# Laying model-width vectors with 8 neighbours in a partition: longer weight runs, column loads of x and c, and a result stored from columns

## Chip, cores and metric

One core of a Trainium2 chip. The metric is the device time of one execution in microseconds (us); executions of one kernel agree within about 0.3%. The time lies about 1.8 us above the span that the profile shows. The profiled run of the kernel before is one of its slowest (444.45 us, span 442.7); its usual span is 442.0 to 442.6.

## The reference, cut to what matters

One decoding step of a transformer block for one token. The model width D is 1024. The work is a modulation, attention over a cache of 65,536 positions with 4 key/value heads, and a gated feed-forward layer; every weight is read once.

```python
mod = silu(c) @ w_mod                                  # w_mod 1024 x 6144
sa, ca, ga, sb, cb, gb = six chunks of 1024
h = layernorm(x) * (1 + ca) + sa
x = x + ga * (attention(h @ wq, k_cache, v_cache) @ wo)  # wq 1024 x 4096, wo 4096 x 1024
h = layernorm(x) * (1 + cb) + sb
x = x + gb * ((gelu(h @ w_gate) * (h @ w_up)) @ w_down)  # 1024 x 3584, twice; 3584 x 1024
```

All arrays are bf16, together 185.6 MB, of which the caches are 134 MB.

## The kernel before

Weights and cache tiles go through ten slots of 16 KB per partition in SBUF, the core's working memory of 128 partitions. One queue of loads runs as far ahead as free slots allow.

```python
x_row = sb("x_row", [KD, P], dt.bfloat16)      # KD = 8, P = 128
c_row = sb("c_row", [KD, P], dt.bfloat16)
# ... some thirty further tiles ...
y_col = sb("y_col", [P, KD])
y_row = sb("y_row", [KD, P], dt.bfloat16)
# ...
slots = [nc.alloc_sbuf_tensor(f"slot{i}", [P, SLOT], dt.bfloat16) for i in range(NSLOT)]
```

The slots come after all the small tiles.

A vector of width 1024 lies so that element `128*k + p` is in partition `p`, column `k`. The rows of a weight matrix are loaded to match, and a product is made block by block: a 128 x 128 piece of weights is the stationary operand and one column of the vector moves, giving 128 results in the partitions.

```python
wq_v = A_wq.rearrange("(k p) n -> p k n", p=P)
# ...
def matvec(bank, jobs, rhs, ready, nblk, pick=None, first=True):
    PE.wait(*ready)
    for (jb, view, k0, nk) in jobs:
        PE.wait(jb.tok)                                  # the tile has landed
        for kk in range(nk):
            for j in range(nblk):
                w = pick(view, kk, j) if pick else view[:, kk, j * P:(j + 1) * P]
                ins = pe.matmul(bank[:, j:j + 1], w, rhs[:, k0 + kk:k0 + kk + 1], ...)
        tok = PE.done(ins)
        release(jb, tok)                                 # the slot may be loaded again
```

Gate and up already use a `pick` that takes every fourth column of the weights. The end of the kernel turns the result from columns to 8 rows and stores those:

```python
v = matvec(acc_bank["dn"], j_d, u_col, (v_uc,), KD)
# ... t_dn = dn * gb; y_col = t_dn + x1_col ...
v = PE.done(pe.transpose(b6[0:KD, 384:384 + P], y_col[:, :], identf[:, :]))
v = DVE.done(dve.tensor_copy(y_row[:, :], b6[0:KD, 384:384 + P]))
sp.dma_start(out[0, 0].rearrange("(j p) -> j p", p=P), y_row[:, :])
```

## Time and profile before

| | before |
|---|---|
| median time | 443.99 us (443.78 to 444.12, 3 runs) |
| DMA packets, bytes | 15,392, 186.08 MB |
| DMA rate from 60 to 360 us | 430 GB/s |
| last full down tile can be used at | 436.83 us |
| end of span | 442.7 us |

The page of the kernel before. The second and third lines cut the span into 40 slices: the busy share of the core's 16 DMA engines in tenths, then GB/s. The last two are the chain of waits that ended last.

```profile
span 442.7 us, 16779 instructions
...
DMA  8999999999999999999999999999999999999994
GB/s 329 429 423 426 434 431 426 429 427 421 432 429 432 426 427 437 432 429 428 434 434 430 429 429 433 431 434 429 429 434 431 432 429 428 423 424 424 427 425 177
DMA packets 15392, 186.08 MB, mean 420 GB/s; under 512 B 1536, under 2 KB 1536, under 8 KB 3840
...
DMA 75%; PE 20%; issue 2%; DVE 1%; SPq 1%; ACT 1%
```

There is no slice without DMA work. The kernel moves bytes all the time, and everything else only matters if it changes how fast or how early the bytes move, or if it follows the last bytes.

The timeline of the tensor engine in the feed-forward layer: start and duration in us, engine, line, output and operands, count, and in brackets how long the engine had been idle and what ended that.

```profile
392.59 2.02 PE L316 MATMUL kt_ps<-h_col,slot 128*128 128x1 bf16 x56 [2.01 <-DVE h_col L363]
...
426.74 1.84 PE L316 MATMUL kt_ps<-u_col,slot 128*128 128x1 bf16 x64 [3.03 <-DMA slot<-in_B_w_down_dram]
```

The first line is one gate tile, with weight columns 4 apart: 56 matmuls in 2.02 us. One matmul lasts 172 ns, but they overlap; from start to start it is (2.02 - 0.172) / 55, or about 34 ns. The second is a down tile with neighbouring columns: (1.84 - 0.165) / 63, or 27 ns.

The end of the same timeline:

```profile
436.83 2.29 PE L316 MATMUL kt_ps<-u_col,slot 128*128 128x1 bf16 x80 [3.45 <-DMA slot<-in_B_w_down_dram]
439.28 0.58 PE L316 MATMUL kt_ps<-u_col,slot 128*128 128x1 bf16 x16 [0.15 <-DMA slot<-in_B_w_down_dram]
439.90 0.17 DVE L664 TENSOR_TENSOR t_dn<-kt_ps,mod_sb 128x8 f32<-128x8 f32 x1 [15.91 <-PE kt_ps L316]
440.10 0.17 DVE L666 TENSOR_TENSOR y_col<-t_dn,x_col 128x8 f32<-128x8 f32 x1
440.32 0.38 PE L668 MATMUL b<-identf,y_col 128*8 128x128 f32 x1 [0.46 <-DVE y_col L666]
440.74 0.28 DVE L670 CAST y_row<-b 8x128 bf16<-8x128 f32 x1 [0.47 <-PE b L668]
441.04 0.37 SPq L672 DMA_DIRECT2D out_dram<-y_row  x1
```

After the last full down tile there are 96 matmuls (the last 16 wait for the last small tile), then 1.14 us from the first vector instruction to the issue of the store, and 1.6 us from there to the end of the span.

Two waits in the timeline and in the wait list, which the change touches: x and c landed at 6.79 us, and the last wait of the store queue (in all, times, longest) was for the store to land.

```profile
6.79 0.16 PE L296 MATMUL b<-ident,c_row 8*128 8x8 bf16 x1 [6.79 <-DMA x_row<-in_A_x_dram]
```

```profile
SPq L676 <- DMA out_dram<-y_row: 0.9, 1, 0.9
```

### The profile page before, as it was taken

How to read it: one execution, taken by the hardware profiler on the slowest of the kernel's cores; microseconds unless marked ns; L12 is line 12 of the kernel's file. 1: busy time of each engine (PE TensorE's matmuls, PEld its weight loads, DVE VectorE, ACT ScalarE, POOL GpSimd, SP SyncE). 2: the span in 40 equal slices, each digit the busy share in tenths (PEclk: the TensorE clock that was granted, in tenths of full speed). 3: DMA queues.
4: the chain of work that ended last, by engine and by line, in shares of the span. 5: the costliest groups of instructions: out<-in, count | busy, mean ns of one | idle time of the engine just before them, and what ended most of it. 6: DMA issues, size and time to landing. Idle time of an engine off the chain costs nothing.

```text
span 442.7 us, 16779 instructions
## 1 busy us (share of the span) xinstructions
PE 335.0 (76%) x7849; PEld 325.2 (73%) x7849; DVE 164.8 (37%) x282; ACT 143.1 (32%) x548; POOL 3.8 (1%) x21
## 2 busy tenths in 40 slices
PE   1333468898979899989899988979898974654434
PEld 1333458898979899979799987969898964654434
DVE  1000046544536445544644644554544443210000
ACT  1000013444444333634533453543343562000000
POOL 2000000000000000000000000000000000000000
PEclk9999999867788956967955996895967785555555
DMA  8999999999999999999999999999999999999994
GB/s 329 429 423 426 434 431 426 429 427 421 432 429 432 426 427 437 432 429 428 434 434 430 429 429 433 431 434 429 429 434 431 432 429 428 423 424 424 427 425 177
DMA packets 15392, 186.08 MB, mean 420 GB/s; under 512 B 1536, under 2 KB 1536, under 8 KB 3840
## 3 DMA queue, kind: packets, MB, share of 16 engines
q1 hardware_dynamic: 15328, 185.61, 98.5%
q8 instruction: 25, 0.41, 0.3%
q14 instruction: 7, 0.06, 0.0%
q10 hardware_dynamic: 32, 0.00, 0.0%
HBM read 185.60 MB, written 0.00 MB: 419 GB/s over the span
## 4 chain that ended last, share of the span: by engine, by line
DMA 75%; PE 20%; issue 2%; DVE 1%; SPq 1%; ACT 1%
DMA slot<-in_A_v_cache_dram 55%; PE kt_ps L417 9%; DMA slot<-in_A_wq_dram 8%; DMA slot<-in_B_w_up_dram 6%; DMA slot<-in_B_w_down_dram 6%; PE b L481 5%; PE sc_ps L437 3%; PE kt_ps L316 1%; SPq L212 1%; PE b L461 1%; ACT p_sb L547 1%; PE b L451 1%; DVE kt_sb L612 0%; PE b L621 0%; DVE zs L597 0%
## 5 line engine op out<-in xcount | busy, mean ns | idle before, releaser
L417 PE MATMUL kt_ps<-ident,slot 128*128 128x128 bf16 x2048 | 171.9, 252 | 4.9 <-DMA slot<-in_A_k_cache_dram 3.0
L516 DVE COPY kt_sb<-kt_ps 128x2048 bf16<-128x2048 bf16 x96 | 117.5, 1225 | 100.0 <-PE kt_ps L417 99.7
L417 PEld LDWEIGHTS kt_ps<-ident,slot 128*128 128x128 bf16 x2048 | 148.6, 114 | 6.6 <-issue 4.2
L516 ACT ACTIVATE kt_sb<-kt_ps 128x2048 bf16<-128x2048 bf16 x32 | 60.1, 1878 | 217.7 <-PE kt_ps L417 217.7
L481 PE MATMUL b<-p_sb,slot 128*128 128x8 bf16 x2048 | 71.0, 167 | 29.5 <-DMA slot<-in_A_v_cache_dram 20.9
L481 PEld LDWEIGHTS b<-p_sb,slot 128*128 128x128 bf16 x2048 | 65.1, 100 | 32.2 <-DMA slot<-in_A_v_cache_dram 22.2
L547 ACT ACTIVATE p_sb<-sc_ps,mneg 128x64 bf16<-128x64 f32 x256 | 83.6, 560 | 5.7 <-DVE mneg L542 5.7
L547 ACT ACTIVATION_READ_ACCUMULATOR p_sb<-sc_ps,mneg 128x1 f32 x256 | 77.2, 364 | 0.0
L437 PE MATMUL sc_ps<-q_buf,kt_sb 128*128 128x8 bf16 x2048 | 67.4, 167 | 0.1
L437 PEld LDWEIGHTS sc_ps<-q_buf,kt_sb 128*128 128x128 bf16 x2048 | 65.1, 100 | 0.2 <-issue 0.2
L316 PE MATMUL kt_ps<-h_col,slot 128*128 128x1 bf16 x448 | 16.2, 172 | 16.9 <-DMA slot<-in_B_w_up_dram 9.1
L316 PEld LDWEIGHTS kt_ps<-h_col,slot 128*128 128x128 bf16 x448 | 15.6, 118 | 17.6 <-DMA slot<-in_B_w_up_dram 9.4
L316 PE MATMUL sc_ps<-s_col,slot 128*128 128x1 bf16 x384 | 11.5, 165 | 15.8 <-DMA slot<-in_w_mod_dram 15.8
L535 DVE TENSOR_REDUCE m_col<-sc_ps 128x8 f32<-128x512 f32 x32 | 21.8, 681 | 4.4 <-PE sc_ps L437 4.4
L316 PEld LDWEIGHTS sc_ps<-s_col,slot 128*128 128x128 bf16 x384 | 11.0, 105 | 16.4 <-DMA slot<-in_w_mod_dram 16.4
L540 DVE TENSOR_REDUCE mg<-b 8x1 f32<-8x128 f32 x32 | 8.9, 279 | 34.4 <-PE b L451 34.4
L316 PE MATMUL sc_ps<-h_col,slot 128*128 128x1 bf16 x256 | 7.4, 165 | 12.6 <-DMA slot<-in_A_wq_dram 12.6
L316 PEld LDWEIGHTS sc_ps<-h_col,slot 128*128 128x128 bf16 x256 | 7.1, 104 | 12.9 <-DMA slot<-in_A_wq_dram 9.3
L461 PE MATMUL b<-negi,mg 8*128 8x8 f32 x64 | 15.0, 304 | 0.4 <-DVE mg L540 0.4
L461 PEld LDWEIGHTS b<-negi,mg 8*128 8x128 f32 x64 | 12.0, 233 | 2.6 <-DVE mg L540 0.6
L316 PE MATMUL kt_ps<-u_col,slot 128*128 128x1 bf16 x224 | 6.6, 165 | 9.6 <-DMA slot<-in_B_w_down_dram 9.6
L316 PEld LDWEIGHTS kt_ps<-u_col,slot 128*128 128x128 bf16 x224 | 6.3, 104 | 9.9 <-DMA slot<-in_B_w_down_dram 6.8
(74 smaller groups left out, 63.2 us busy)
## 6 DMA issues: line engine op xcount, KB each, us to landing
slot<-in_A_k_cache_dram SPq DMA_DIRECT2D x32, 2048.0 KB, 29.6
slot<-in_A_v_cache_dram SPq DMA_DIRECT2D x32, 2048.0 KB, 33.2
slot<-in_w_mod_dram SPq DMA_DIRECT2D x8, 1536.0 KB, 19.0
slot<-in_A_wq_dram SPq DMA_DIRECT2D x4, 2048.0 KB, 37.0
slot<-in_A_wo_dram SPq DMA_DIRECT2D x4, 2048.0 KB, 34.7
slot<-in_B_w_gate_dram SPq DMA_DIRECT2D x4, 1792.0 KB, 39.4
slot<-in_B_w_up_dram SPq DMA_DIRECT2D x4, 1792.0 KB, 29.0
slot<-in_B_w_down_dram SPq DMA_DIRECT2D x3, 2048.0 KB, 30.4
```

Source lines behind the costliest of these rows:

```text
L212: sp.dma_start(j.view, j.src).then_inc(j.tok[0], 16)
L316: ins = pe.matmul(bank[:, j:j + 1], w, rhs[:, k0 + kk:k0 + kk + 1], start=first, stop=True, skip_group_check=True,)
L417: ins = pe.transpose(kt_ps[:, half * 2048 + t * P:half * 2048 + (t + 1) * P], j_k[i].view[:, b * TB + t, :], ident[:, :],)
L437: ins = pe.matmul(sc_ps[:, base + n * REP:base + (n + 1) * REP], kt_sb[:, j % 2, n, :], q_buf[:, j % SITES, :], start=True, stop=True,)
L451: ins = pe.transpose(b6[0:REP, 32:32 + P], m_col[:, j % 2, :], identf[:, :]) if emit else None
L461: ins = pe.matmul(b6[:, 256:256 + REP], mg8[:, j % 2:j % 2 + 1].to_broadcast([REP, P]), negi[:, :], start=True, stop=True,)
L481: ins = pe.matmul(b7[:, s * REP:(s + 1) * REP], j_v[j].view[:, n, :], p_sb[:, s, n, :], start=(n == 0), stop=(n == CH - 1),)
L516: ev[i % SITES][b].done(act.activation(dst, src, ACT.Copy) if E_ is AC else dve.tensor_copy(dst, src))
L535: m1[s].done(dve.tensor_reduce(m_col[:, j % 2, :].unsqueeze(2), scv, AX.X, ALU.max))
L540: m2[s].done(dve.tensor_reduce(mg8[:, j % 2:j % 2 + 1], b6[0:REP, 32:32 + P], AX.X, ALU.max))
L547: ins = act.activation(p_sb[:, s, :, h], scv[:, h, :], ACT.Exp, bias=mneg[:, j, h:h + 1], scale=scale, accum_out=z_all[:, j, h:h + 1],)
```

## The change

Element `8*p + k` of a width-1024 vector now lies in partition `p`, column `k`. A partition then needs 8 neighbouring weight rows, so two rows of a tile are one run in memory: 16 KB in place of two of 8 KB for the q weights, 14 KB in place of two of 7 KB for gate and up. x and c can be loaded as columns (16 bytes to each partition), and the result can be stored from columns without a transpose. In return, the stages that produce width-1024 vectors must take every eighth weight column (`pick_d`). The last down tile is split into 3 and 1 rows instead of 2 and 2.

```diff
-    x_row = sb("x_row", [KD, P], dt.bfloat16)
-    c_row = sb("c_row", [KD, P], dt.bfloat16)
+    x_in = sb("x_in", [P, KD], dt.bfloat16)
+    c_in = sb("c_in", [P, KD], dt.bfloat16)
...
-    y_col = sb("y_col", [P, KD])
-    y_row = sb("y_row", [KD, P], dt.bfloat16)
+    y_col = sb("y_col", [P, KD], dt.bfloat16)
...
-        wmod_v = w_mod.rearrange("(k p) n -> p k n", p=P)
-        wq_v = A_wq.rearrange("(k p) n -> p k n", p=P)
+        wmod_v = w_mod.rearrange("(p k) n -> p k n", p=P)
+        wq_v = A_wq.rearrange("(p k) n -> p k n", p=P)
...            (gate and up the same; x and c loaded with "(p k) -> p k")
-            for e in range(0, UE, 2):
+            for e, ne in ((0, UE - 1), (UE - 1, 1)):
...
-        pe.matmul(b6[:, 0:KD], c_row[:, :], ident[0:KD, 0:KD], start=True, stop=True)
...            (the two small transposes of c and x at the start go)
+        def pick_d(view, kk, j):
+            m, e = divmod(j, KD)
+            return view[:, kk, m * D:(m + 1) * D].rearrange("p (m e) -> p e m", e=KD)[:, e, :]
...            (used for the modulation, the output projection and down)
-        v = matvec(acc_bank["dn"], j_d, u_col, (v_uc,), KD)
+        v = matvec(acc_bank["dn"], j_d, u_col, (v_uc,), KD, pick_d)
...
-        v = PE.done(pe.transpose(b6[0:KD, 384:384 + P], y_col[:, :], identf[:, :]))
-        v = DVE.done(dve.tensor_copy(y_row[:, :], b6[0:KD, 384:384 + P]))
-        sp.dma_start(out[0, 0].rearrange("(j p) -> j p", p=P), y_row[:, :])
+        sp.dma_start(out[0, 0].rearrange("(p k) -> p k", p=P), y_col[:, :])
```

More of the change, by code (lines that the diff above doesn't have):

```diff
@@ L225, in emit_all @@
     def emit_all():
-        act.dma_start(c_row[:, :], c[0].rearrange("(j p) -> j p", p=P)).then_inc(in_sem, 16)
-        act.dma_start(x_row[:, :], A_x[0, 0].rearrange("(j p) -> j p", p=P)).then_inc(in_sem, 16)
-        wmod_v = w_mod.rearrange("(k p) n -> p k n", p=P)
-        wq_v = A_wq.rearrange("(k p) n -> p k n", p=P)
+        act.dma_start(c_in[:, :], c[0].rearrange("(p k) -> p k", p=P)).then_inc(in_sem, 16)
+        act.dma_start(x_in[:, :], A_x[0, 0].rearrange("(p k) -> p k", p=P)).then_inc(in_sem, 16)
+        wmod_v = w_mod.rearrange("(p k) n -> p k n", p=P)
+        wq_v = A_wq.rearrange("(p k) n -> p k n", p=P)
         wo_v = A_wo.rearrange("(p k) n -> p k n", p=P)
-        wg_v = B_w_gate.rearrange("(k p) n -> p k n", p=P)
-        wu_v = B_w_up.rearrange("(k p) n -> p k n", p=P)
+        wg_v = B_w_gate.rearrange("(p k) n -> p k n", p=P)
+        wu_v = B_w_up.rearrange("(p k) n -> p k n", p=P)
         wd_v = B_w_down.rearrange("(b p e) n -> p b e n", p=P, e=UE)
@@ L260, in emit_all @@
         b = 0
-        while b + 2 < NBF:
+        while b + 2 <= NBF - 1:
             jb = plan_load(
@@ L269, in emit_all @@
         while b < NBF:
-            for e in range(0, UE, 2):
-                jb = plan_load(wd_v[:, b, e:e + 2, :], flat(2, D), next(tail))
-                j_d.append((jb, jb.view, b * UE + e, 2))
+            for e, ne in ((0, UE - 1), (UE - 1, 1)):
+                jb = plan_load(wd_v[:, b, e:e + ne, :], flat(ne, D), next(tail))
+                j_d.append((jb, jb.view, b * UE + e, ne))
             b += 1
@@ L293, in emit_all @@
         v_negi = DVE.done(dve.tensor_scalar(negi[:, :], identf[0:REP, 0:REP], -scale, None, ALU.mult))
-        PE.wait(t1, (in_sem, 32))
-        pe.matmul(b6[:, 0:KD], c_row[:, :], ident[0:KD, 0:KD], start=True, stop=True)
-        v_ct = PE.done(pe.matmul(b6[:, KD:2 * KD], x_row[:, :], ident[0:KD, 0:KD], start=True, stop=True))
-        AC.wait(v_ct)
-        v_th = AC.done(act.activation(th_col[:, :], b6[:, 0:KD], ACT.Tanh, scale=0.5))
-        DVE.wait(v_ct, v_th)
-        v_x = DVE.done(dve.tensor_copy(x_col[:, :], b6[:, KD:2 * KD]))
+        AC.wait((in_sem, 32))
+        v_th = AC.done(act.activation(th_col[:, :], c_in[:, :], ACT.Tanh, scale=0.5))
+        DVE.wait(v_th, (in_sem, 32))
+        v_x = DVE.done(dve.tensor_copy(x_col[:, :], x_in[:, :]))
         v = DVE.done(dve.tensor_scalar(sg_col[:, :], th_col[:, :], 0.5, 0.5, ALU.mult, ALU.add))
         DVE.wait(v)
-        v_s = DVE.done(dve.tensor_tensor(s_col[:, :], b6[:, 0:KD], sg_col[:, :], ALU.mult))
+        v_s = DVE.done(dve.tensor_tensor(s_col[:, :], c_in[:, :], sg_col[:, :], ALU.mult))
         def matvec(bank, jobs, rhs, ready, nblk, pick=None, first=True):
@@ L363, in modulate @@
             return DVE.done(dve.tensor_tensor(out_t[:, :], ht[:, :], mod_sb[:, off_s:off_s + KD], ALU.add))
+        def pick_d(view, kk, j):
+            m, e = divmod(j, KD)
+            return view[:, kk, m * D:(m + 1) * D].rearrange("p (m e) -> p e m", e=KD)[:, e, :]
         OFF = [i * KD for i in range(6)]
         hn1, v_hn1 = ln_norm("1", x_col[:, :], v_x, 16)
-        v = matvec(acc_bank["mod"], with_view(j_mod), s_col, (v_s,), MD)
+        v = matvec(acc_bank["mod"], with_view(j_mod), s_col, (v_s,), MD, pick_d)
         DVE.wait(v)
@@ L629, in emit_all @@
         last_ev = tuple(ev[(NC - 1) % SITES][b].tok(seen_by(NC - 1)) for b in range(NB))
-        v = matvec(acc_bank["att"], with_view(j_o), o_pk, (v_opk,) + last_ev, KD)
+        v = matvec(acc_bank["att"], with_view(j_o), o_pk, (v_opk,) + last_ev, KD, pick_d)
         t_att = sb("t_att", [P, KD])
@@ L666, in emit_all @@
         v = DVE.done(dve.tensor_tensor(y_col[:, :], t_dn[:, :], x1_col[:, :], ALU.add))
-        PE.wait(v)
-        v = PE.done(pe.transpose(b6[0:KD, 384:384 + P], y_col[:, :], identf[:, :]))
-        DVE.wait(v)
-        v = DVE.done(dve.tensor_copy(y_row[:, :], b6[0:KD, 384:384 + P]))
         SP.wait(v)
-        sp.dma_start(out[0, 0].rearrange("(j p) -> j p", p=P), y_row[:, :]).then_inc(out_sem, 16)
+        sp.dma_start(out[0, 0].rearrange("(p k) -> p k", p=P), y_col[:, :]).then_inc(out_sem, 16)
         sp.wait_ge(out_sem, 16)
```

## The prediction

> **What bounds the kernel now.** The DMA. The page's forty slices show its engines at 8-9 tenths throughout; the windows view gives a DMA share of 1.0 from 5 to 432 us; the chain of waits is 75% DMA. So extra compute before 430 us costs nothing if slots are released in time. What counts: packets per DMA engine, the start, and what follows the last landings.
>
> **What the change moves, priced.**
>
> 1. Fewer packets. The trace's DMA packet records: 611 ns for 16384 B, 309 for 8192, 272 for 7168, 159 for 4096, so about 9 ns fixed plus 27.2 GB/s. The q weights go from two 8 KB runs to one of 16 KB, gate and up from two of 7 KB to one of 14 KB: 96 packets fewer per engine at 7-8 ns (estimate from these durations), -0.7 us; the 16-byte pieces of x and c give 0.1 back. On the critical path: -0.6 us.
>
> 2. Start. x landed at 6.8 us. The Trainium skill, "DMA: Bandwidth & Descriptors", section "Queues, rings and completion order", says each engine takes its queue rows in turn, packet by packet. The records agree: between x's packet and its semaphore write lie 0.47 us, one 12 KB packet. With 8 pieces per engine x should land near 10-11 us (estimate). The modulation starts 3 us later and catches up: the q weights land only at 39.2 us. Worth 0.
>
> 3. Weights read with a step of 8 columns (16 bytes) in modulation, output projection and down. The timeline: 64 unit-step down matmuls in 1.87 us (27 ns from start to start), 56 gate matmuls of step 4 in 2.03 us (34 ns). The skill, "SBUF — State Buffer", section "Door 1: The DMA port swizzle", gives SBUF 16-byte lines and a penalty for each access to a new line. The trace agrees that a step costs (27 to 34 ns). With step 8 every column is a new line: 67 ns if cost is proportional to lines, 40 if the penalty adds; I take 50 (estimate). Modulation (2.4 us per 3.65 us tile) and projection (6 us later, caught up before the up tiles at 408.8 us) stay hidden. Down does not: its last full tile lands at 436.8 us and 96 matmuls follow, 96 x (50 - 27) = +2.2 us, less 0.3 that the old kernel spent waiting for its last tile: +1.9 (range +0.4 to +3.5).
>
> 4. Tail. Transpose and row copy go: y is ready at 440.27 us instead of 441.02, -0.75 us. The store becomes 128 pieces of 16 bytes: +0.2 us (guess).
>
> 5. A last tile of 8 matmuls instead of 16: 0 if PE is behind.
>
> Sum: -0.6 + 1.9 - 0.75 + 0.2 = +0.8 us. **Predicted 444.8 us, 80% range 443.0 to 446.6.** Faster by over 2% 0.01, within 2% 0.97, slower by over 2% 0.02.
>
> **What would show it.** About 14,240 packets, those under 512 B near 1,920. Down, modulation and projection matmuls 40-67 ns apart, gate and up unchanged. The chain ends in down matmuls with no DMA wait before the last tile. x lands at 10-11 us; DMA share still 1.0 from 5 to 430 us. Last down matmul to end of span about 2.2 us instead of 2.8.
>
> **What would make it wrong.** A step of 8 that costs no more than 4 (then 443.2), or far more than 67 ns; a DMA rate changed by partitions reading addresses 56-96 KB apart; a slow store of 16-byte pieces.

## The result, and the profile after

| | before | after |
|---|---|---|
| median time | 443.90 us (5 runs) | 450.66 us (450.34 to 450.83, 5 runs) |
| ratio | | 1.0151 (95%: 1.0138 to 1.0165) |
| DMA packets | 15,392 | 14,241 |
| DMA rate from 60 to 360 us | 430 GB/s | 427 GB/s |
| last full down tile can be used at | 436.83 us | 439.53 us |
| end of span | 442.7 us | 448.8 us |

A ratio is the mean time of one kernel's fast runs over that of the other's of the same rounds, so not quite the ratio of the medians quoted. The change costs 6.8 us. The prediction said 0.8 more, and at most 2.6 more. The result is correct.

The page of the kernel after, same lines as shown of before:

```profile
span 448.8 us, 16772 instructions
...
DMA  8999999999999999999999999999999999999991
GB/s 332 426 426 426 429 425 421 428 424 421 426 423 429 431 424 426 431 426 429 429 426 430 429 424 429 429 426 430 428 428 429 427 428 426 424 426 423 416 400 68
DMA packets 14241, 186.08 MB, mean 415 GB/s; under 512 B 1921, under 2 KB 1921, under 8 KB 2177
...
issue 86%; DMA 10%; PE 2%; DVE 0%; POOLq 0%; POOL 0%; ACTq 0%; ACT 0%
```

The packet counts are as predicted and the DMA still never rests, but it is a little slower in nearly every slice. The chain of waits is of no use here: one step lands on an instruction of the GpSimd engine at 13.9 us whose engine then has nothing for 387 us, and all of that is booked as "issue". A chain that is 86% "issue" has lost the thread; the slices and the timeline have to be read instead.

The timeline of the tensor engine after, at the start and in the output projection, gate and last down stages:

```profile
27.35 3.06 PE L313 MATMUL sc_ps<-s_col,slot 128*128 128x1 bf16 x48 [0.31 <-DMA slot<-in_w_mod_dram]
...
382.92 15.53 PE L313 MATMUL kt_ps<-o_pk,slot 128*128 128x1 bf16 x256 [0.29 <-DVE o_pk L628]
...
401.77 7.71 PE L313 MATMUL kt_ps<-h_col,slot 128*128 128x1 bf16 x224 [2.00 <-DVE h_col L360]
411.75 2.02 PE L313 MATMUL kt_ps<-h_col,slot 128*128 128x1 bf16 x56 [2.26 <-DMA slot<-in_B_w_up_dram]
```

Start to start, a matmul with step 8 takes (3.06 - 0.198) / 47, or 61 ns, in the modulation, and 60 ns in the projection. Both remain hidden: a modulation tile of 3.06 us still waits for the next one (0.31 us idle), and after the longer projection the four gate tiles are worked off in one go (224 matmuls, 34 ns each as before), so that the engine waits 2.26 us for the first up tile again.

The end of the timeline after:

```profile
439.53 5.94 PE L313 MATMUL kt_ps<-u_col,slot 128*128 128x1 bf16 x96 [0.94 <-DMA slot<-in_B_w_down_dram]
445.51 0.17 DVE L665 TENSOR_TENSOR t_dn<-kt_ps,mod_sb 128x8 f32<-128x8 f32 x1 [18.55 <-PE kt_ps L313]
445.71 0.17 DVE L667 TENSOR_TENSOR y_col<-t_dn,x_col 128x8 bf16<-128x8 f32 x1
445.91 0.35 SPq L669 DMA_DIRECT2D out_dram<-y_col  x1
```

Three differences stand here. The last full tile comes 2.7 us later (439.53 against 436.83). The 96 matmuls take 5.94 us in place of 3.03 (436.83 to 439.86). From the store's issue to the end of the span it is 2.9 us in place of 1.6, while the way from the products to the store has shrunk from 1.14 to 0.40 us. The wait for the store, and the arrival of x:

```profile
SPq L673 <- DMA out_dram<-y_col: 2.1, 1, 2.1
```

```profile
11.17 0.21 ACT L296 ACTIVATE th_col<-c_in 128x8 f32<-128x8 bf16 x1 [8.24 <-DMA x_in<-in_A_x_dram]
```

**Where the first difference comes from.** The trace records every DMA packet with its size and duration. Counted for the queue of the weights and caches:

```
packet size     before: count, median, mean ns     after: count, median, mean ns
16384 B         8704   611   612.1                 9216   613   616.0
14336 B            -                               1024   538   541.5
12288 B         1024   460   470.3                 1024   460   473.2
 8192 B         1792   309   310.1                  768   312   315.1
sum, with x, c and the store, per engine: 436.2 us        438.5 us
```

The cache loads were not touched by the change, and yet their packets take about 4 ns longer in the mean: before, 99.5% of the 16 KB packets take exactly 611 ns; after, 98% of them spread from 611 to 621. Something that the diff does not name had changed for them. In the program as built it is the place of the slots: `x_row`, `c_row` and `y_row` take 256 bytes in every partition, though they use only 8 of the partitions; `x_in` and `c_in` take 32, and `y_row` is gone. So all slots moved down by 2 x 224 + 256 = 704 bytes. Slot 0 started at byte 62208, which is 243 x 256; it now starts at 61504, which is 240 x 256 + 64. Slots are 16384 bytes apart, so all ten are off the 256-byte grid in the same way.

The Trainium skill, "DMA: Bandwidth & Descriptors", section "How a descriptor splits into AXI transactions", says that a transfer is split into transactions of 256 bytes, and that one which does not start on a 256-byte address begins with a transaction at the boundary below, whose unused bytes still cost beats (pieces of 32 bytes); it says this of reads. That made the place of the slots the first theory to test.

### The profile page after: what moved, and what is told of

Same layout as the page of the kernel before. It is cut to its first block, busy times and chain, and to the rows that moved or that the text cites. A ratio compares the mean times of both kernels' runs of the same rounds, so it can differ in the third digit from the quotient of the medians.

```text
span 448.8 us, 16772 instructions
## 1 busy us (share of the span) xinstructions
PE 363.5 (81%) x7846; PEld 354.5 (79%) x7846; DVE 164.6 (37%) x281; ACT 143.1 (32%) x548; POOL 3.7 (1%) x21
## 2 busy tenths in 40 slices
DMA packets 14241, 186.08 MB, mean 415 GB/s; under 512 B 1921, under 2 KB 1921, under 8 KB 2177
## 4 chain that ended last, share of the span: by engine, by line
issue 86%; DMA 10%; PE 2%; DVE 0%; POOLq 0%; POOL 0%; ACTq 0%; ACT 0%
DMA slot<-in_B_w_down_dram 8%; DMA x_in<-in_A_x_dram 2%; PE kt_ps L313 2%; POOLq L673 0%; PE b L338 0%; POOL rs L348 0%; ACTq L226 0%; DVE hn L350 0%; ACT th_col L296 0%; DVE t_dn L665 0%; DVE h_col L360 0%; DVE ht L357 0%; DVE va L345 0%; DVE me L340 0%; DVE sq L342 0%
## 5 line engine op out<-in xcount | busy, mean ns | idle before, releaser
L418 PE MATMUL kt_ps<-ident,slot 128*128 128x128 bf16 x2048 | 173.9, 253 | 7.8 <-DMA slot<-in_A_k_cache_dram 3.5
L418 PEld LDWEIGHTS kt_ps<-ident,slot 128*128 128x128 bf16 x2048 | 150.3, 115 | 9.7 <-issue 7.0
L313 PEld LDWEIGHTS sc_ps<-s_col,slot 128*128 128x128 bf16 x384 | 23.6, 162 | 1.8 <-DMA slot<-in_w_mod_dram 1.8
L313 PE MATMUL sc_ps<-s_col,slot 128*128 128x1 bf16 x384 | 23.7, 198 | 1.6 <-DMA slot<-in_w_mod_dram 1.6
L313 PE MATMUL kt_ps<-u_col,slot 128*128 128x1 bf16 x224 | 13.9, 198 | 4.9 <-DMA slot<-in_B_w_down_dram 4.9
L313 PEld LDWEIGHTS kt_ps<-u_col,slot 128*128 128x128 bf16 x224 | 13.7, 164 | 5.1 <-issue 3.1
L313 PE MATMUL kt_ps<-o_pk,slot 128*128 128x1 bf16 x256 | 15.5, 198 | 0.3 <-DVE o_pk L628 0.3
L313 PEld LDWEIGHTS kt_ps<-o_pk,slot 128*128 128x128 bf16 x256 | 15.5, 170 | 0.4 <-DVE o_pk L628 0.4
```

What stands on the lines that cost most here:

```text
L418: ins = pe.transpose(kt_ps[:, half * 2048 + t * P:half * 2048 + (t + 1) * P], j_k[i].view[:, b * TB + t, :], ident[:, :],)
```

## The experiments

Theory: (a) the place of the slots slows every packet, worth 3 to 4 us; (b) step 8 in the 96 down matmuls, about 3 us; (c) the store of 16-byte pieces, about 1.2 us; less the transpose and the saved packets. Rivals: the memory dislikes the new row distances; the modulation and projection are what costs; the end of the span is a fixed latency.

### e1_after_aligned: put the slots back on the grid

```diff
+    sb("pad", [P, 176])            # 704 bytes per partition
     slots = [nc.alloc_sbuf_tensor(f"slot{i}", ...
```

> The kernel after, with a dummy tensor of 704 bytes per partition ahead of the ten weight slots, so that slot 0 starts again at byte 62208 (a multiple of 256) as in the kernel before, not at 61504 (64 over a multiple of 256). Nothing else changes. Theory (where the slots start in SBUF sets the time of each packet): the 16384-byte packets go back from 613 to 611 ns at the median and from 616 to 612 in the mean, the last full down tile lands near 436.2 us instead of 439.5, and the time falls by about 3.3 us to near 447.3. Rival (the memory is slower because partitions now read addresses 56 to 96 KB apart, or this is a drift between runs): packets stay at 613, time stays at 450.6.

Measured: 446.87 us against 444.16 of the kernel before in the same job, ratio 1.0064 (1.0050 to 1.0078). The 16384-byte packets are back at 611 ns median and 612.1 mean, and the sum per engine is 435.7 us, 0.4 below the kernel before. The windows view over the cache loads (PE, PEld, DVE, ACT, POOL busy; granted clock; DMA share; GB/s), first after, then e1:

```profile
60.00:360.00 300.00, 272.87 (x5923) 266.02 (x5922) 149.89 (x226) 133.97 (x511) 0.00 (x0) 0.80 1.01 427
```

```profile
60.00:360.00 300.00, 271.22 (x5972) 264.79 (x5971) 151.41 (x227) 134.08 (x511) 0.00 (x0) 0.82 1.01 430
```

And the last full tile in e1:

```profile
435.94 5.94 PE L314 MATMUL kt_ps<-u_col,slot 128*128 128x1 bf16 x96 [1.00 <-DMA slot<-in_B_w_down_dram]
```

It comes at 435.94 us, 3.6 us earlier than in the kernel after. Over its own kernel before, the loss falls from 6.76 us (450.66 - 443.90) to 2.71 (446.87 - 444.16): the place of the slots is worth 4.05 us. The new row distances in memory are the same in both, so that rival falls.

### e2_before_shifted: take the slots off the grid in the kernel before

```diff
+    sb("pad", [P, 16])             # 64 bytes
     slots = [...
```

> The kernel before, with a dummy tensor of 64 bytes per partition ahead of the slots, so that slot 0 starts at 62272, 64 over a multiple of 256, as in the kernel after. Theory: packets of 16384 bytes go to 613 ns median, 616 mean; time 443.9 + 3.3 = about 447.2. Rival (the slowdown came with the new weight layout or a drift): stays at 443.9.

Measured: 448.15 us, ratio 1.0090 (1.0076 to 1.0103), so 3.99 us more. Packets 613 median, 615.9 mean. The same 4 us as in e1, from the other side, with nothing else of the change present. The rate over the cache loads (same columns as above) falls as in the kernel after:

```profile
60.00:360.00 300.00, 270.35 (x5901) 264.04 (x5900) 149.38 (x225) 133.82 (x511) 0.00 (x0) 0.81 1.01 427
```

My figure of 3.3 was low: I had taken the sum of the packets of the mean engine. That sum rises by 3.4 us here (439.6 against 436.2). Where the rest of the 3.99 comes from is not shown; the engine that ends last may be slower than the mean one. The 25 packets of the queue for instructions grew too, from 934 to 1,069 ns at the median.

### e6_before_shift128 and e7_before_shift224: how far off the grid?

The same edit with 128 and with 224 bytes.

> The kernel before with slot 0 at 128 over a multiple of 256. If a write that starts off the 256-byte grid wastes the beats below its start, as the account of the skill has it for reads, the 16384-byte packets grow with the offset: about 4 to 5 ns over 611 against 2 (median) at 64, and the time to 449 or more. If any offset costs the same one extra piece: like e2, 613 ns median and 448.1 us.

> The kernel before with slot 0 at 224 over a multiple of 256. Growing with the offset: 8 ns over 611 and about 451 us or more. The same for any offset: like e2, 613 ns median and 448.1 us.

Measured: 447.94 us (ratio 1.0083) and 449.13 us (1.0108), against 444.20. Mean packet 615.7 and 616.8 ns, against 615.9 at 64 and 612.1 at 0. An offset of 128 is no dearer than one of 64, so a cost that grows with the bytes below the start is not what this shows; 224 costs 1 us more than either, far from the 7 us of that idea. Being off the grid at all is the larger part. In two further kernels below, with slot 0 at 62976 and at 63488 (246 and 248 times 256), the median is 611 again.

### e3_aligned_unit_down: e1 with neighbouring columns in the down stage

```diff
-        v = matvec(acc_bank["dn"], j_d, u_col, (v_uc,), KD, pick_d)
+        v = matvec(acc_bank["dn"], j_d, u_col, (v_uc,), KD)
```

> e1 with the down projection reading its weight columns with step 1 instead of 8 (the result is wrong on purpose). Theory (step 8 costs 60 ns per matmul instead of 27, and only the 96 down matmuls after the last full tile are on the critical path): those 96 take about 2.7 us instead of 5.9, the time falls by about 3 us from e1, to near 444.0. Modulation and output projection keep step 8 here; if they cost time as well, this run stays well above 444. Rival (the late start of the modulation or the longer projection is what costs): e3 is no faster than e1.

Measured: 443.94 us, ratio 0.9998; the result is wrong. The step costs 446.87 - 443.94 = 2.93 us in the down stage. The tail of e3:

```profile
435.96 2.86 PE L314 MATMUL kt_ps<-u_col,slot 128*128 128x1 bf16 x96 [3.09 <-DMA slot<-in_B_w_down_dram]
```

The tile comes at the same time as in e1 (435.96), the 96 matmuls take 2.86 us in place of 5.94. Modulation and projection still have step 8 here and x is as late, and yet the tile comes no later than in the kernel before (436.83; 436.44 in the profile of e9): there they cost nothing that can be seen.

### e4_aligned_row_store: e1 with a store of 8 rows

```diff
-        sp.dma_start(out[0, 0].rearrange("(p k) -> p k", p=P), y_col[:, :])
+        sp.dma_start(out[0, 0].rearrange("(j p) -> j p", p=P), y_fake[:, :])   # 8 x 128 zeros
```

> e1 with the final store taken from an 8 x 128 tile of zeros, 8 rows of 256 bytes as before, in place of 128 pieces of 16 bytes (the result is wrong on purpose); it waits for the same instruction. Theory (the store of small pieces takes 2.9 us from issue to the end of the span against 1.6): time falls by about 1.25 us from e1, to near 446.0. Rival (the end of the span is a fixed latency): no change from e1.

Measured: 445.80 us, ratio 1.0037: 1.07 us less than e1 (the result is wrong). The wait for the store is back to 0.9 us:

```profile
SPq L676 <- DMA out_dram<-y_fake: 0.9, 1, 0.9
```

So the small pieces cost more than the transpose that they replace (1.14 - 0.40 = 0.74 us). In the packet records the 128 pieces leave as early after the issue as the 8 rows do, at 9 ns each; the extra time lies after the packets, until the completion is seen. Why is not shown.

### e8_steps: the law of the column step

```diff
+            def pick(view, kk, j):
+                return view[:, kk, j:j + (P - 1) * st + 1:st]
#   st = 2 in q, 5 in the projection, 6 in gate, 7 in up, 16 in the modulation
```

> e1 with other column steps in five stages (the result is wrong on purpose), to get the law of the cost: step 2 in the q projection, 5 in the output projection, 6 in gate, 7 in up, 16 in the modulation; down keeps 8. Known so far, start to start: 27 ns at step 1, 34 at 4, 60 at 8. [...]27 at step 2, about 42 at 5, 50 at 6, 58 at 7, and 16 no dearer than 8 (60 to 67). If it grows with the distance itself, 16 costs about twice 8.

The figures for steps 2 to 16 in the expectation are forecasts; the law behind them is cut out of it. The result is wrong, as intended; the time, 447.3 us, is a single look. Its timeline:

```profile
34.07 3.13 PE L314 MATMUL sc_ps<-s_col,slot 128*128 128x1 bf16 x48 [0.52 <-DMA slot<-in_w_mod_dram]
39.00 1.85 PE L314 MATMUL sc_ps<-h_col,slot 128*128 128x1 bf16 x64 [1.80 <-DMA slot<-in_A_wq_dram]
...
380.51 10.40 PE L314 MATMUL kt_ps<-o_pk,slot 128*128 128x1 bf16 x256 [0.29 <-DVE o_pk L634]
...
399.89 2.80 PE L314 MATMUL kt_ps<-h_col,slot 128*128 128x1 bf16 x56 [0.21 <-DMA slot<-in_B_w_gate_dram]
...
408.37 3.16 PE L314 MATMUL kt_ps<-h_col,slot 128*128 128x1 bf16 x56 [1.44 <-DMA slot<-in_B_w_up_dram]
```

From start to start (the group's time less one matmul's 0.165 to 0.2 us, over the count less one):

| step, columns | 1 | 2 | 4 | 5 | 6 | 7 | 8 | 16 |
|---|---|---|---|---|---|---|---|---|
| ns per matmul | 27 | 27 | 34 | 40 | 47 | 54 | 60 | 62 |

Between 4 and 8 each further column of distance costs about 6.6 ns, and past 8 hardly anything; the forecasts for 5, 6 and 7 (42, 50 and 58) were somewhat too high. The stages ran at different granted clocks (the share of its full speed that the tensor engine is allowed), 1.00 for steps 2 and 16 and 0.50 for 5 to 8, but that does not decide it: in the kernel after, step 8 costs 61 ns at 1.00 (modulation) and 60 at 0.50 (projection), and in the kernel before step 1 costs 27 at either. Eight bf16 columns are 16 bytes, the line of SBUF that the Trainium skill names ("SBUF — State Buffer", section "Door 1: The DMA port swizzle"). So the cost would follow the number of lines touched, which cannot rise past one per column: the measurement fits that reading, though no run separates it from other causes that stop at 16 bytes. The prediction's two candidates for step 8 were 67 and 40 ns; the measured 60 lies between, near the first.

### e9_before_split31: the other split alone

```diff
-            for e in range(0, UE, 2):
+            for e, ne in ((0, UE - 1), (UE - 1, 1)):
```

> The kernel before with only the change's other split of the last down tile: 3 and 1 rows of weights in place of 2 and 2. Theory: the last landing is followed by 8 step-1 matmuls instead of 16, 8 x 27 ns = 0.2 us less, so about 0.1 to 0.2 us below the kernel before. Rival (the smaller runs of 2 KB cost, or the instructions before it decide): no change or slower.

Measured: 443.72 us against 443.92, ratio 0.9994 (0.9981 to 1.0008). As expected in size, but inside the interval of no change.

### e5_both_layouts: keep the longer runs, end as before

A correct version. x, one gate and the output projection are made in both layouts, so that the down stage can use neighbouring columns and the row store; slots aligned.

```diff
+            if m < 5: return pick_d(view, kk, j)          # modulation: step 8 for five chunks,
+            base = (5 if m == 5 else 2) * D + e * P       # step 1 for gb and for a second ga
...
-        v = matvec(acc_bank["att"], with_view(j_o), o_pk, ..., KD, pick_d)
+        v = matvec(acc_bank["att"], with_view(j_o), o_pk, ..., 2 * KD, pick_att)
```

> A correct version that keeps the longer runs and the aligned slots, but does the last stage as the kernel before did: the down weights are read with step 1, the result goes through the transpose and is stored as 8 rows of 256 bytes. For that x, one gate of the modulation and the output projection are made in both layouts (256 more projection matmuls and 64 more of modulation, in stages where the DMA is ahead). Theory: these extra matmuls cost nothing, the DMA stream ends 0.7 to 0.9 us earlier than before, the last full down tile is followed by step-1 matmuls: about 443.0, 0.9 below the kernel before. Rival (the modulation and projection with step 8 are on the path): 445 or more.

Measured: 444.74 us against 444.20, ratio 1.0015 (1.0001 to 1.0029). A miss: it is not faster. The matmuls in the tail behave, but the last full tile is late again:

```profile
437.14 2.84 PE L324 MATMUL kt_ps<-u_col,slot 128*128 128x1 bf16 x96 [3.11 <-DMA slot<-in_B_w_down_dram]
```

437.14 us against 435.94 in e1, although the packets are as fast (611 ns) and their sum per engine is the same (435.7 us). The records also show packets that fetch instructions on the same DMA engines: 28 of 16 KB in e5, 25 in e1, at 934 ns median.

### e10_aligned_extra_matmuls: do hidden matmuls cost DMA time?

```diff
-        v = matvec(acc_bank["att"], with_view(j_o), o_pk, ..., KD, pick_d)
+        v = matvec(acc_bank["att"], with_view(j_o), o_pk, ..., KD + 10, pick_extra)   # 320 more, unread
```

> e1 with 320 more matmuls of step 1 in the output projection, whose results nobody reads. e5 had as many more matmuls, hidden behind the DMA, and yet its last full down tile landed 1.2 us later than in e1, though the sum of the packet times was the same; it had 28 instruction packets of 16 KB on the DMA engines instead of 25. Theory (more instructions are more fetches, and a fetch of about 0.93 us on the engine that ends last delays the end): 28 fetches, the tile lands about 1 us later, time near 447.9. Rival (the three loads at the start of e5, or its longer stall before the gate stage): as e1, 446.9.

Measured: 448.77 us (448.29 to 449.52) against 443.92, ratio 1.0114; over its own kernel before that is 2.1 us more than e1 (4.85 against 2.71). In the profile the last full tile comes at 437.34 us, 1.4 later than in e1:

```profile
437.34 5.93 PE L314 MATMUL kt_ps<-u_col,slot 128*128 128x1 bf16 x96 [0.38 <-DMA slot<-in_B_w_down_dram]
```

There are 27 fetches, not 28. Following each engine's last packets by time (counted from the first weight packet):

```
e1    25 fetches   8 engines end at 431.7-433.8 us, 8 at 435.8-436.2
e5    28 fetches   3 engines end at 437.3-437.4, the others as in e1
e10   27 fetches   2 engines end at 437.6-437.7, the others as in e1 (up to 436.4)
```

So extra matmuls do cost time although the tensor engine has room for them: shown. It is not that the longer projection frees the slots too late: in e10 the last load is issued at 415.1 us, over 20 us before its tile is used, and until 432 us at least 15 of its packets are under way at any time. That it is their fetches, landing on engines that end last, fits these records but is not shown; the records carry no engine number, and some 0.7 us of e10's 2.1 is in no profile that I have (the profiled run was its fastest).

### e11_shuffled_x1: the same goal with few instructions

Correct. As e5, but x after attention is brought into the other layout by 8 small matmuls with a selection matrix in a stage where the tensor engine waits.

```diff
+        for k in range(KD):
+            ins = pe.matmul(b6[:, 400:400 + KD], Eext[:, KD - k:KD - k + P], xr[:, k, :],
+                            start=(k == 0), stop=(k == KD - 1))
```

> A correct version like e5 but almost without extra matmuls: one gate chunk of the modulation is read with step 1, and x after attention is brought into the other layout by 8 small matmuls with a selection matrix after the gate stage. Down with step 1, transpose and row store as before, longer runs, slots aligned. Theory: the last full down tile lands at about 435.9 us as in e1, step-1 matmuls follow, time about 443.1, 1.0 below the kernel before. Rival (the gain of the longer runs is not there without a change of something else): 444 or more.

Measured: 443.49 us (443.46 to 443.87) against 443.92, ratio 0.9992 (0.9978 to 1.0006). There are 25 fetches, and the last full tile comes on time:

```profile
435.97 2.84 PE L327 MATMUL kt_ps<-u_col,slot 128*128 128x1 bf16 x96 [3.10 <-DMA slot<-in_B_w_down_dram]
```

Its median is the lowest of all kernels here, 0.4 us below the kernel before and 0.2 below e9, but the interval includes no change. The 1.0 us that I expected was too much: I had started from the profile of the kernel before, whose run was about 0.5 us slower than its median.

## Why the prediction was wrong, point by point

Differences are of medians, each over its own kernel before or within one job, in us.

| term | predicted | measured | from |
|---|---|---|---|
| fewer packets (and the split) | -0.6 | -0.55 | what is left of e1's +2.71 after the three next terms (the packet sums fall by 0.4) |
| step 8 in the down stage | +1.9 | +2.93 | e1 less e3 |
| transpose and copy gone | -0.75 | -0.74 | timelines: 1.14 to 0.40 |
| store in 16-byte pieces | +0.2 | +1.07 | e1 less e4 |
| slots moved in SBUF | not in the sum | +4.05 | +6.76 less e1's +2.71; e2 alone: +3.99 |
| sum | +0.8 | +6.76 | |

- **What bounds the kernel.** Right. In every run the DMA share was about 1.0 until the last tiles, and whatever lengthened the packets came through to the time. What was drawn from it, that extra compute before 430 us costs nothing if slots are released in time, did no harm here (the change adds no matmuls), but e10 refutes it: 320 hidden matmuls cost 2.1 us.
- **Point 1, fewer packets: the step that failed.** "Fewer packets ... On the critical path: -0.6 us". The saving was real, but the step took the packet durations of the trace as fixed and counted packets only. They depend on where in SBUF the packets land. The removal of the three row tiles moved the slots 64 bytes off the 256-byte grid, and the 9,216 packets of 16 KB grew by about 4 ns in the mean: +4.05 us in the time, of the 6.0 by which the sum was missed. I had named "a DMA rate changed" as a danger, but blamed the addresses in memory, not those in SBUF.
- **Point 2, the start.** Right, a little low: x landed at 11.17 us (predicted 10 to 11), worth nothing (e3).
- **Point 3, step 8.** The mechanism and the place were right; the term was mis-sized. Per matmul it is 60 ns, not 50, and the sum is 2.93 in place of 2.2 (1.9 after the 0.3 us of waiting that was taken off; e1 less e3 contains no such wait), inside the stated range of 0.4 to 3.5. That modulation and projection stay hidden was right.
- **Point 4, the tail.** The saving was right (0.74 against 0.75 us). The store, called a guess, was five times too low, and with its real price this part of the change is a loss.
- **Point 5, the split.** In line with e9: 0.2 at most. In e1 the engine is behind, so it waits for no last tile there.

Without the moved slots the result would have been 443.9 + 2.7 = 446.6 us, the top edge of the range, a rise of 2.7 where 0.8 was forecast: the two mis-sized terms, step 8 and the store, err in the same direction. The slots carried it well past that.

## What to carry to other kernels

When the DMA never rests, look at the durations of packets that the change does not touch: if they move, look for a cause that the lines of the diff do not name, such as where things lie. Here a few bytes of padding settled it. Removing or adding any small tile can move large buffers; keep the buffers that DMA fills on a 256-byte grid, by padding as in e1 or otherwise. A layout that spares work at one end has to be charged at the other: here the longer runs saved about 0.6 us and the missing transpose 0.7, and the strided weights and small store pieces that paid for them cost 4.0.

## What the Trainium skill lacked or had wrong

- "DMA: Bandwidth & Descriptors", section "How a descriptor splits into AXI transactions", speaks of reads and of beats wasted below the start. It names no price for the SBUF address that a load writes to, and the runs show one: 16384-byte packets of 612.1 ns in the mean on the 256-byte grid, 615.9, 615.7 and 616.8 ns at offsets of 64, 128 and 224 bytes, and 4.0, 3.7 and 4.9 us over the kernel. It does not grow in step with the offset.
- "SBUF — State Buffer", section "Door 1: The DMA port swizzle", lets one stride "for free" up to 8 bf16. For the weights of a matmul with one moving column that is not so: step 2 is free (27 ns), 4 costs 34 ns, 8 costs 60 and 16 costs 62. Nor are the two hits per line that it asks for enough: step 4 still has two, and pays.
- No page that I found gives the cost of a small final store by its pieces: 128 pieces of 16 bytes ended 1.07 us later than 8 of 256 bytes.
- No page that I found gives what the fetching of instructions costs the other traffic of DMA engines that never rest. Here 25 packets of 16 KB take 934 ns each at the median, and 320 hidden matmuls more made the kernel 2.1 us slower (that the fetches are the cause is not shown).
